# Decode attention with a gated MLP: four heads per load, 32 KB per partition, instead of one head per load

## The chip, the core and the metric

The kernel runs on one core of a Trainium2 chip. It is written by hand in instruction streams, one for each engine: TensorE (PE in the profile; PEld is its weight loads), VectorE (DVE), ScalarE (ACT), GpSimd (POOL) and SyncE (SP). The streams meet only at semaphores. SP, ACT and POOL also issue DMA transfers, which run on the core's 16 DMA engines. The metric is device time in microseconds, the median of several runs: lower is better.

## The reference

One token `x` of 512 features is decoded against a cache of 32 heads with 4096 keys and 4096 values of 128 features each (bfloat16), and goes through a small MLP. The two results are mixed by a gate:

```python
def _A_ref(x, k_cache, v_cache, wq, wo):          # wq 512x4096, wo 4096x512
    q = (x @ wq) per head                         # 32 heads of 128
    scores = jnp.einsum("bhqd,bhkd->bhqk", q, k) * (Dh ** -0.5)
    p = _softmax(scores, axis=-1)
    o = jnp.einsum("bhqk,bhkd->bhqd", p, v)
    return o.reshape(B, Sq, Hq * Dh) @ wo
...
def _B_ref(x, w1, b1, w2, b2):                    # w1 512x1376, w2 1376x512
    h = relu(x @ w1 + b1) ** 2
    return h @ w2 + b2
...
g = _sigmoid((x * gate_w).sum(-1, keepdims=True))
return g * a + (1 - g) * b
```

Every key and every value is used once. They are 67.1 MB of the 78.8 MB that the kernel reads.

## The kernel before, in words

**Tiling.** A head's 4096 keys lie on 128 partitions as 32 blocks of 128 keys: partition p holds keys 32p to 32p+31, which are 8 KB in a row in memory. One DMA loads one head's keys (1 MB, `load_k`, L259), one its values (`load_v`, L265). Keys have 8 buffers (`Kt`, NK), values 8 (`Vt`, NV).

**Scores** are made in two ways. DVE multiplies the first 16 blocks with the query, which `qb` holds alike on all partitions, and sums over the features (`ttr`, L631, one instruction per block, XB = 16). For the other 16 blocks PE transposes each block into PSUM (L428, banks `KP`), ACT copies eight of them at a time to SBUF (`evac`, L362), and PE multiplies each with the query as a column (`scores`, L439). DVE copies these 16 scores beside its own (`smax`, L637) and takes the maximum.

**Softmax.** For four heads at a time PE transposes the maxima (`max_rows`), DVE reduces them (`gmax`), PE spreads them again (`max_cols`), and ACT makes the exponentials and their sums (`exps`, L373).

**Values.** `pv` (L464) multiplies each of the 32 blocks of values with its column of exponentials, 32 matmuls with one column each. `den` sums the denominators, `norm` (L658) divides and applies the gate.

**Queries.** wq comes first, in four loads of 1 MB. `q_rows(c)` (L406) makes the queries of four heads as rows on all partitions (four matmuls of 512 columns), ACT copies them to `qb` (L354), `q_cols` (L414) makes the four columns, and DVE copies them to `qcol`. The columns of wq are done step by step along the heads; `q_rows(7)` is done near the 19th head.

**Output.** The rows of wo for heads 0 to 22 are brought into the room of wq once all queries are made (`s_qps`), as strips of rows: fourteen strips (`RUNS`) by POOL, each row in pieces of 8 KB, with small dummy loads between them (`xb<-in_B_w_dram`, L316), and five strips (`FIRST`) by SP. POOL then waits for the dummies and for `mlp_h`, clears `w1_sb` and builds the selection matrices in it (L326 to L334). `turn_a` and `spread_a` bring the outputs of the first heads into the order of these rows (head 23 has its own step, `out_x`, L532); `out_a` (L508) multiplies 23 of the 32 row groups on PE, `part_y` the other nine on DVE (L681), and `sum_y` adds them. Heads 24 to 31 go through `regroup` and `out_b` (L526). The MLP is `mlp_h` (L478, L482), `mlp` on DVE and `mlp_out` (L547). All sums meet in `acc`, four columns of 128. At the end DVE adds the bias, PE transposes the four columns into four rows (L594), DVE copies them, and SP sends them (L295).

**Order.** Every stream is a loop over the heads written out by hand. SP loads seven heads of keys, then values and keys in turn:

```python
for h in range(LAG):
    load_k(h)
for h in range(NH):
    load_v(h)
    if h + LAG < NH:
        load_k(h + LAG)
```

A load into a used buffer waits on SP until DVE and PE are done with the old keys (`s_sd`, `s_t`) or PE with the old values (`s_pv`), and all later loads wait behind it.

Of the kernel before, what the change touches and what calls it, by code (L numbers as in the profile page):

```python
# [5 lines left out]
def bass_gated_mix__gqa_block_cached__dense_activation_squared_relu__decode_kernel(  # L6
# [15 lines left out]

# [7 lines left out]
    NB = 32  # L35
# [7 lines left out]
    XB = 16  # L43
    YB = NB - XB
    HB = YB // 2
    NK = 8
    NV = 8
    NS = 12
    NE = 8
    G = 4  # L50
    NG = NH // G
    HPO = 8
    LAG = 7
    NA = 24
    TB = 8
    GS = [0, 8, 10]
    TD = 23
# [9 lines left out]
    HF = 20  # L67
# [26 lines left out]
    k_h = A_k_cache.rearrange("a h (p b) d -> (a h) p (b d)", p=128)  # L94
    v_h = A_v_cache.rearrange("a h (p b) d -> (a h) p (b d)", p=128)
    wq_v = A_wq.rearrange("(p t) n -> p t n", t=4)
    woa_v = A_wo.rearrange("(p t) n -> p (t n)", t=32)
    wob_v = A_wo[NA * 128:NH * 128, :].rearrange("(p t) n -> p (t n)", t=TB)
# [4 lines left out]
    with ctx:  # L103
# [8 lines left out]

        Kt = sb("Kt", [128, NK, NB * 128], bf16)
        Vt = sb("Vt", [128, NV, NB * 128], bf16)
# [3 lines left out]
        wox = Kt[:, 1, 0:DM]  # L118
        wob_sb = Kt[:, 0, :].rearrange("p (t n) -> p t n", t=TB)
        qb = sb("qb", [128, NH * 128], bf16)  # L120
        kT = sb("kT", [128, 2, YB * 128], bf16)
# [24 lines left out]
        E = sb("E", [128, NE, NB], bf16)  # L146
        mp = sb("mp", [128, NH], fp32)
        gm = sb("gm", [G, NG], fp32)
        dg = sb("dg", [G, NG, G], fp32)
        nM = sb("nM", [128, NH], fp32)  # L150
# [9 lines left out]
        hs = sb("hs", [128, FG + 1], bf16)  # L160
        b2g = sb("b2g", [128, 4], fp32)
        fin = sb("fin", [128, 4], bf16)

        KP = [pb(f"KP{i}", [128, HB * 128], bf16) for i in range(3)]
        pS = pb("pS", [128, 512], fp32)
        pM = pb("pM", [128, 512], fp32)
        pO = pb("pO", [128, 512], fp32)
        pX = pb("pX", [128, 512], fp32)
        pQ = pb("pQ", [128, 512], fp32)
        S2 = pS[:, 0:YB]  # L170
        O2A = pS[:, 64:96]
        O2B = pS[:, 128:128 + TB]
        o2D = S[:, NS - 1, 0:32 - TD]
        yD = kT[:, 0, 0:1024].bitcast(fp32)
        MT = pM[:, 0:128]
        MB = pM[:, 128:128 + NH]
        DEN = pM[:, 192:192 + NH]
        Z = pX[:, 0:1]
        XC = pO[:, 0:4]
        Q = pQ[:, 0:4]  # L180
        H = pX[:, 128:128 + FG + 1]
        acc = pX[:, 256:260]
        OB = [pO, pX, pO, pQ]

        def O(a, b):
            c = a // HPO
            return OB[c][:, 320 + a - HPO * c:320 + b - HPO * c]

        s_wr = sem("s_wr")
        s_wx = sem("s_wx")  # L190
        s_y = sem("s_y")
        s_y2 = sem("s_y2")
        s_x = sem("s_x")
        s_dz = sem("s_dz")
        s_b = sem("s_b")
        s_wq = [sem(f"s_wq{t}") for t in range(4)]
        s_w1 = sem("s_w1")
        s_w2 = [sem(f"s_w2{n}") for n in range(len(GS))]
# [3 lines left out]
        s_at = sem("s_at")  # L202
        s_ac = sem("s_ac")
        s_sb = sem("s_sb")
        s_b2 = sem("s_b2")
        s_oT = sem("s_oT")
        s_oc = sem("s_oc")
        s_o2 = sem("s_o2")
        s_fT = sem("s_fT")
        s_f4 = sem("s_f4")  # L210
        s_k = [sem(f"s_k{i}") for i in range(NK)]
        s_v = [sem(f"s_v{i}") for i in range(NV)]
        s_id = sem("s_id")
        s_cst = sem("s_cst")
        s_xc = sem("s_xc")
# [5 lines left out]
        s_g = sem("s_g")  # L221
        s_q = sem("s_q")
# [21 lines left out]
        s_hs = sem("s_hs")  # L244
        s_acc = sem("s_acc")
        s_fin = sem("s_fin")
        s_out = sem("s_out")

        nc.sync.dma_start(wq_sb[:, 0, :], wq_v[:, 0, :]).then_inc(s_wq[0], 16)
# [5 lines left out]
        def _(eng):  # L255
            for t in range(1, 4):
                eng.dma_start(wq_sb[:, t, :], wq_v[:, t, :]).then_inc(s_wq[t], 16)

            def load_k(h):  # L259
                if h >= NK:  # L260
                    eng.wait_ge(s_sd, h - NK + 1)
                    eng.wait_ge(s_t, 2 * (h - NK + 1))
                eng.dma_start(Kt[:, h % NK, :], k_h[h, :, :]).then_inc(s_k[h % NK], 16)  # L263

            def load_v(h):  # L265
                if h >= NV:
                    eng.wait_ge(s_pv, h - NV + 1)
                eng.dma_start(Vt[:, h % NV, :], v_h[h, :, :]).then_inc(s_v[h % NV], 16)  # L268

            for h in range(LAG):  # L270
                load_k(h)
            for h in range(NH):
                load_v(h)
                if h + LAG < NH:
                    load_k(h + LAG)
                if h == HF:
                    eng.wait_ge(s_qps, 8)
                if HF <= h < HF + len(FIRST):
                    p, st, k, q = STRIPS[len(RUNS) + h - HF]
                    eng.dma_start(W[p:p + st * (k - 1) + 1:st, :], woa_v[q:q + k, :],  # L280
                                  max_dma_last_dim=8192).then_inc(s_wr, 16)
                if h == 8:
                    eng.wait_ge(s_z, 1)
                    eng.wait_ge(s_b2, 1)
                    for t in range(4):
                        eng.dma_start(w1_sb[:, t, :], w1_v[:, t, :]).then_inc(s_w1, 16)
# [53 lines left out]
        def _(eng):  # L340
# [15 lines left out]
            def evac(h):  # L356
                if h >= 2:
                    eng.wait_ge(s_s2, h - 1)
# [29 lines left out]
        def _(eng):  # L388
# [43 lines left out]
            def scores(h):  # L432
                if h >= 1:
                    eng.wait_ge(s_cp, h)
# [318 lines left out]
```

## Time and profile before

| | |
|---|---|
| median of 3 runs | 196.97 us (196.86 to 197.03) |
| span of the profiled execution | 195.4 us, 6571 instructions |
| moved | 78.76 MB, 403 GB/s over the span |
| PE busy | 132.8 us (68%) |
| DVE busy | 139.5 us (71%) |
| ACT busy | 79.4 us (41%) |
| POOL busy | 29.9 us (15%) |
| DMA's share of the chain that ended last | 59% |

The profile gives the span of the profiled execution, from its first to its last instruction, and no other time of it: the runs' median stands 1.6 us above this span. The 40 slices of the page are 4.9 us each; a digit is the busy share in tenths. PEclk is the clock that TensorE was granted, in tenths. A group of instructions is given with its line, engine, operation, tiles and shapes, then its busy time, the mean nanoseconds of one, and the idle time of the engine just before them with what ended it. An issue of a DMA is given with its count, KB each and median time to landing.

### The profile page before, as it was taken

Reading aid. Unit: us, or ns where it says so; the run is one execution under the profiler, and the core shown is the slowest. Engines: PE = TensorE matmul, PEld = TensorE weight load, DVE = VectorE, ACT = ScalarE, POOL = GpSimd, SP = SyncE. Lnnn points to the kernel's source line nnn. Section 1 sums busy time; section 2 is a strip of 40 time slices with the busy share of each in tenths; the row PEclk is TensorE's granted clock in tenths of the full one; section 3 lists DMA queues with packets and bytes.
Section 4 is the critical chain, followed back from the end, with each engine's and each line's share of the span. In section 5 each row is a group of like instructions: output and inputs, shape, how many; then the busy total and the mean of one; then the engine's idle time right before and its main releaser. Section 6 shows DMA issues by size and latency. Waiting matters only on the chain.

```text
span 195.4 us, 6571 instructions
## 1 busy us (share of the span) xinstructions
PE 132.8 (68%) x2409; PEld 117.3 (60%) x2409; DVE 139.5 (71%) x1151; ACT 79.4 (41%) x148; POOL 29.9 (15%) x53
## 2 busy tenths in 40 slices
PE   0128657597986857906797771568998677787774
PEld 0106527476686647606667761568997667776664
DVE  0307999999998687707877773577769999958510
ACT  2105838456563536403347330633068333612000
POOL 2000000000000000000009950000089760000000
PEclk9999966667555665555555555555555555555555
DMA  6999999999999999999999999999999999999991
GB/s 227 420 426 424 424 418 424 411 421 426 416 411 423 418 421 407 420 421 421 418 421 419 411 416 416 406 409 413 408 419 421 426 409 421 419 423 414 416 382 57
DMA packets 12717, 78.76 MB, mean 403 GB/s; under 512 B 2489, under 2 KB 2715, under 8 KB 3356
## 3 DMA queue, kind: packets, MB, share of 16 engines
q1 hardware_dynamic: 11134, 75.77, 94.0%
q0 software_dynamic: 1536, 2.56, 3.5%
q8 instruction: 19, 0.31, 0.7%
q14 instruction: 14, 0.11, 0.2%
q10 hardware_dynamic: 14, 0.01, 0.0%
HBM read 78.32 MB, written 0.00 MB: 401 GB/s over the span
## 4 chain that ended last, share of the span: by engine, by line
DMA 59%; DVE 22%; PE 9%; SPq 6%; issue 3%; ACT 0%
DMA Kt<-in_A_k_cache_dram 42%; DVE Kt L631 19%; DMA w2a<-in_B_w_dram 12%; DMA W<-in_A_wq_dram 6%; SPq L268 4%; PE KP L428 3%; PE pX L482 2%; DVE S L631 1%; SPq L263 1%; PE pQ L406 1%; PE pX L478 1%; PE pX L547 1%; PE pS L439 1%; DVE dg L646 1%; DVE S L637 0%
## 5 line engine op out<-in xcount | busy, mean ns | idle before, releaser
L631 DVE CUSTOM_DVE_ANT_0 Kt<-Kt,qb 128x128 bf16<-128x128 bf16 x512 | 113.3, 290 | 23.4 <-DMA Kt<-in_A_k_cache_dram 23.4
L362 ACT ACTIVATE kT<-KP 128x1024 bf16<-128x1024 bf16 x64 | 61.8, 1021 | 68.4 <-PE KP L428 68.4
L428 PE MATMUL KP<-ident,Kt 128*128 128x128 bf16 x512 | 55.2, 294 | 32.0 <-DMA Kt<-in_A_k_cache_dram 32.0
L428 PEld LDWEIGHTS KP<-ident,Kt 128*128 128x128 bf16 x512 | 47.9, 137 | 34.4 <-DMA Kt<-in_A_k_cache_dram 33.6
L631 DVE DVE_READ_ACCUMULATOR2_ANT S<- 128x1 f32 x512 | 41.4, 81 | 0.0
L439 PE MATMUL pS<-qcol,kT 128*128 128x1 bf16 x512 | 19.0, 167 | 11.1 <-DVE S L637 11.1
L439 PEld LDWEIGHTS pS<-qcol,kT 128*128 128x128 bf16 x512 | 18.4, 106 | 13.2 <-DVE S L637 13.2
L316 POOL DMA_DIRECT2D xb<-in_B_w_dram x9 | 5.3, 592 | 100.3 <-PE pQ L406 100.3
L406 PE MATMUL pQ<-W,xb 128*128 128x512 bf16 x32 | 14.5, 609 | 6.4 <-DMA W<-in_A_wq_dram 6.4
L464 PEld LDWEIGHTS pO<-E,Vt 128*128 128x128 bf16 x512 | 15.4, 104 | 1.1 <-issue 0.8
L464 PE MATMUL pO<-E,Vt 128*128 128x1 bf16 x512 | 16.0, 165 | 0.0
L334 POOL TENSOR_SCALAR_AFFINE_SELECT w_sb<-w_sb 24x36 bf16<-24x36 bf16 (+5 forms) x19 | 11.0, 577 | 2.7
L354 ACT ACTIVATE qb<-pQ 128x512 bf16<-128x512 f32 x8 | 4.7, 591 | 14.8 <-PE pQ L406 14.8
L406 PEld LDWEIGHTS pQ<-W,xb 128*128 128x128 bf16 x32 | 3.6, 130 | 10.9 <-issue 10.9
L373 ACT ACTIVATE E<-S,nM 128x32 bf16<-128x32 f32 x32 | 9.9, 309 | 0.3
L464 PE MATMUL pQ<-E,Vt 128*128 128x1 bf16 x256 | 8.1, 165 | 2.3 <-DMA Vt<-in_A_v_cache_dram 2.0
L464 PEld LDWEIGHTS pQ<-E,Vt 128*128 128x128 bf16 x256 | 7.7, 104 | 2.6 <-issue 2.5
L464 PEld LDWEIGHTS pX<-E,Vt 128*128 128x128 bf16 x256 | 7.9, 105 | 0.7 <-issue 0.6
L464 PE MATMUL pX<-E,Vt 128*128 128x1 bf16 x256 | 8.1, 166 | 0.0
L319 POOL DMA_DIRECT2D W<-in_A_wo_dram x14 | 7.8, 563 | 0.0
L617 DVE CAST qcol<-pQ 128x4 bf16<-128x4 f32 x8 | 1.2, 152 | 8.5 <-PE pQ L414 8.5
L637 DVE COPY S<-pS 128x16 f32<-128x16 f32 x32 | 5.4, 169 | 2.2 <-PE pS L439 2.2
(85 smaller groups left out, 93.5 us busy)
## 6 DMA issues: line engine op xcount, KB each, us to landing
Kt<-in_A_k_cache_dram SPq DMA_DIRECT2D x32, 1024.0 KB, 27.1
Vt<-in_A_v_cache_dram SPq DMA_DIRECT2D x32, 1024.0 KB, 27.2
W<-in_A_wq_dram SPq DMA_DIRECT2D x4, 1024.0 KB, 7.8
W<-in_A_wo_dram POOLq DMA_DIRECT2D x2, 768.0 KB, 13.0
w_sb<-in_B_w_dram SPq DMA_DIRECT2D x4, 344.0 KB, 22.9
Kt<-in_A_wo_dram SPq DMA_DIRECT2D x1, 1024.0 KB, 21.5
w2a<-in_B_w_dram SPq DMA_DIRECT2D x1, 1024.0 KB, 23.4
W<-in_A_wo_dram POOLq DMA_DIRECT2D x10, 64.0 KB, 23.4
```

The source lines that it names most:

```text
L268: eng.dma_start(Vt[:, h % NV, :], v_h[h, :, :]).then_inc(s_v[h % NV], 16)
L316: eng.dma_start(dm[0:d, sent, :, 0:8], src[:, :, 0:8]).then_inc(s_dm[sent], 16)
L319: eng.dma_start(W[p:p + st * (k - 1) + 1:st, :], woa_v[q:q + k, :], max_dma_last_dim=8192).then_inc(s_wp[n], 16)
L334: eng.affine_select(out=part, in_=part, compare_op=ALU.not_equal, fill=1.0, base=-st * q, pattern=[[st, 4], [-1, st * (k - 1) + 1]], chann ...
L362: eng.activation(kT[:, h % 2, j * HB * 128:(j + 1) * HB * 128], KP[n % 3][:, :], ACT.Copy).then_inc(s_ev, 1)
L373: eng.activation(E[:, h % NE, :], S[:, h % NS, :], ACT.Exp, bias=nM[:, h:h + 1], scale=SCALE, accum_out=RS[:, h:h + 1]).then_inc(s_e, 1)
L406: mm = eng.matmul(pQ[:, :], xb[:, t, :], wq_sb[:, t, c * 512:(c + 1) * 512], start=(t == 0), stop=(t == 3))
L428: mm = eng.transpose(KP[n % 3][:, y * 128:(y + 1) * 128], Kt[:, h % NK, b * 128:(b + 1) * 128], ident[:, :])
L439: mm = eng.matmul(S2[:, y:y + 1], kT[:, h % 2, y * 128:(y + 1) * 128], qcol[:, h:h + 1], start=True, stop=True)
L464: mm = eng.matmul(O(h, h + 1), Vt[:, h % NV, b * 128:(b + 1) * 128], E[:, h % NE, b:b + 1], start=(b == 0), stop=(b == NB - 1))
L631: ins = eng.tensor_tensor_reduce(kb, kb, qb[:, h * 128:(h + 1) * 128], 1.0, 0.0, ALU.mult, ALU.add, S[:, h % NS, b:b + 1])
L637: eng.tensor_copy(S[:, h % NS, XB:NB], S2).then_inc(s_cp, 1)
```

## The change

**Loads.** One DMA loads the keys (or values) of four heads, a quad: head r of the quad lies on partitions 32r to 32r+31, and each partition holds 128 keys in a row, 32 KB. There are 8 quads. One tile `KV` has 4 slots of 32 KB per partition, as much as `Kt` and `Vt` had together: keys go through slots 0 to 2, values through slot 3 alone, but for the last two quads of values, which take slots 2 and 0. The first quad of keys is loaded in four parts, the second in two, the last quad of values in four. The rest of SP's order is in the diff.

**Scores.** DVE takes 14 of each 32 blocks (XB), PE the other 18, in nine groups of eight per quad. A transposed block now has the keys of all four heads; PE multiplies it with four columns at once, and ACT copies from each row group its own head's column (`s_copy`). Exponentials are written with zeros for the other heads, so that `pv` multiplies 128 blocks with four columns each.

**Order.** PE works on group g of a quad and the scores of group g-2; the values of quad q-2 are multiplied after the scores of quad q. Query columns 1 and 2 follow quad 0, 3 to 5 lie in quad 1, 6 and 7 in quad 2 (`Q_AT`). wq comes as its first 512 columns, ahead of the keys, and the rest behind the first quad of keys. POOL's strips follow `q_rows(7)` as before. `mlp_h` follows quad 4.

**End.** `part_y` and `sum_y` are gone; `out_a` does all 32 row groups on PE, ahead of the last quad of values. The last two groups of w2 are multiplied by PE as rows (`mlp_rows`, with `hd` holding the four copies of a column among zeros), in the shape of the output: `acc` with the bias is turned into rows by one FP32 matmul and added to them in PSUM, and DVE copies the rows out.

```diff
-    XB = 16
-    NK = 8
-    NV = 8
-    LAG = 7
-    TD = 23
+    R = 4
+    NQ = NH // R
+    NB = 128
+    NP = 4
+    XB = 14
+    GB = 8
+    GQ = YQ // GB
+    K_PARTS = [[1, 1, 1, 1], [2, 2]] + [[4]] * (NQ - 2)
+    V_PARTS = [[4]] * (NQ - 1) + [[1, 1, 1, 1]]
+    K_SLOT = [q % 3 for q in range(NQ)]
+    V_SLOT = [3] * (NQ - 2) + [2, 0]
+    W2_PARTS = [(0, 4), (4, 8), (FG, FG + 1), (8, 9), (9, 10)]
...
-    k_h = A_k_cache.rearrange("a h (p b) d -> (a h) p (b d)", p=128)
-    v_h = A_v_cache.rearrange("a h (p b) d -> (a h) p (b d)", p=128)
+    k_q = A_k_cache.rearrange("a (q r) (p b) d -> (a q) (r p) (b d)", r=R, p=32)
+    v_q = A_v_cache.rearrange("a (q r) (p b) d -> (a q) (r p) (b d)", r=R, p=32)
...
+            def load_k(q):
+                if q >= 3:
+                    eng.wait_ge(s_sd, q - 2)
+                    eng.wait_ge(s_t, GQ * (q - 2))
+                load(KV, k_q[q, :, :], K_SLOT[q], K_PARTS[q], s_k[q])
+            def load_v(q):
+                if V_SLOT[q] == 3:
+                    if q >= 1:
+                        eng.wait_ge(s_pv, q)
+                else:
+                    eng.wait_ge(s_sd, q)
+                    eng.wait_ge(s_t, GQ * q)
+                load(KV, v_q[q, :, :], V_SLOT[q], V_PARTS[q], s_v[q])
...
+            load_k(0)
+            eng.dma_start(wq_sb[:, :, 512:4096], wq_v[:, :, 512:4096]).then_inc(s_wq[1], 16)
+            load_k(1)
+            load_k(2)
+            load_v(0)
+            eng.wait_ge(s_z, 1)
+            eng.wait_ge(s_b2, 1)
+            eng.dma_start(w1_sb[:, :, :], w1_v[:, :, :]).then_inc(s_w1, 16)
+            for q in range(3, NQ):
+                load_k(q)
+                if q >= 4:
+                    load_first(q - 4)
+                load_v(q - 2)
+            load_first(4)
+            load_v(NQ - 2)
+            load_w2(0)
+            load_v(NQ - 1)
+            eng.wait_ge(s_sd, NQ)
+            eng.wait_ge(s_t, GQ * NQ)
+            eng.dma_start(wob_sb, wob_v).then_inc(s_wo, 16)
+            load_w2(1)
             eng.dma_start(wox, A_wo[HX * 128:NA * 128, :]).then_inc(s_wx, 16)
+            load_w2(2)
+            load_w2(3)
+            load_w2(4)
...
+        Q_AT = {1: (0, GQ - 1), 2: (0, GQ - 1), 3: (1, 0), 4: (1, 3), 5: (1, 6), 6: (2, 0), 7: (2, 3)}
...
+            def s_copy(q):
+                eng.wait_ge(s_s2, GQ * (q + 1))
+                S2 = pS[q % 2][:, 0:YQ * R].rearrange("p (b r) -> p b r", r=R)
+                for r in range(R):
+                    eng.activation(S[rows(r), q % NS, 0:YQ], S2[rows(r), :, r], ACT.Copy).then_inc(s_cp, 1)
...
+            def pv(q):
+                if q >= 1:
+                    eng.wait_ge(s_on, q)
+                else:
+                    eng.wait_ge(s_bg, 1)
+                for j in range(NP):
+                    eng.wait_ge(s_v[q][part_of(V_PARTS[q], j)], 16)
+                    for b in range(PB * j, PB * j + PB):
+                        mm = eng.matmul(O[:, R * q:R * q + R], KV[:, V_SLOT[q], b * 128:(b + 1) * 128],
+                                        E[:, q % NE, COLUMN[b], :], start=(b == 0), stop=(b == NB - 1))
                 mm.then_inc(s_pv, 1)
...
+            def mlp_rows(c):
+                eng.wait_ge(s_w2[c], 16)
+                n = W2_PARTS[c][0]
+                for j in range(4):
+                    mm = eng.matmul(acc4, hd[:, n - 8, 4 * j:4 * j + 4], w2a[:, n, j * 128:(j + 1) * 128],
+                                    start=(n == 8 and j == 0), stop=(n == FG - 1 and j == 3),
+                                    skip_group_check=True)
+                return mm
...
+            for q in range(NQ):
+                for g in range(GQ):
+                    transposes(q, g)
+                    if g >= 2:
+                        scores(q, g - 2)
...
+                scores(q, GQ - 2)
+                scores(q, GQ - 1)
...
+                if q >= 2:
+                    den(q - 2)
+                    pv(q - 2)
+                if q == 4:
                     mlp_h()
+            max_rows(NQ - 1)
+            turn_a()
+            max_cols(NQ - 1)
+            spread_a()
+            den(NQ - 2)
+            pv(NQ - 2)
+            eng.wait_ge(s_hs, 2)
+            out_a()
+            mlp_out(0)
+            den(NQ - 1)
+            pv(NQ - 1)
             regroup()
             out_b()
+            mlp_out(1)
             out_x()
+            mlp_out(2, last=True)
+            eng.wait_ge(s_hs, 3)
+            mlp_rows(3)
+            eng.wait_ge(s_as, 1)
+            eng.matmul(acc4, accs[:, :], identf[:, :], start=False, stop=False, skip_group_check=True)
+            mlp_rows(4).then_inc(s_fin, 1)
```

## The prediction

> **What bounds the kernel now.** I read the page first (busy shares, slices, queues, chain, groups, DMA issues), then the waits of all engines and of SP, then the timeline at the start, around 57 us and at the end, and last the windows.
>
> The slices, and the DMA queues under them:
>
> ```profile
> DVE  0307999999998687707877773577769999958510
> PEclk9999966667555665555555555555555555555555
> DMA  6999999999999999999999999999999999999991
> GB/s 227 420 426 424 424 418 424 411 421 426 416 411 423 418 421 407 420 421 421 418 421 419 411 416 416 406 409 413 408 419 421 426 409 421 419 423 414 416 382 57
> ...
> DMA packets 12717, 78.76 MB, mean 403 GB/s; under 512 B 2489, under 2 KB 2715, under 8 KB 3356
> ...
> q1 hardware_dynamic: 11134, 75.77, 94.0%
> q0 software_dynamic: 1536, 2.56, 3.5%
> ```
>
> Nothing between the first and the last two slices is below nine tenths on the DMA row: the time is one unbroken stream of 78.76 MB at about 420 GB/s, and the kernel ends when its slowest DMA engine ends. No compute engine is the bound: PE is 68% busy, DVE 71%, ACT 41%.
>
> The groups that the change moves, the waits, and the DMA issues:
>
> ```profile
> L631 DVE CUSTOM_DVE_ANT_0 Kt<-Kt,qb 128x128 bf16<-128x128 bf16 x512 | 113.3, 290 | 23.4 <-DMA Kt<-in_A_k_cache_dram 23.4
> L362 ACT ACTIVATE kT<-KP 128x1024 bf16<-128x1024 bf16 x64 | 61.8, 1021 | 68.4 <-PE KP L428 68.4
> L428 PE MATMUL KP<-ident,Kt 128*128 128x128 bf16 x512 | 55.2, 294 | 32.0 <-DMA Kt<-in_A_k_cache_dram 32.0
> ...
> L373 ACT ACTIVATE E<-S,nM 128x32 bf16<-128x32 f32 x32 | 9.9, 309 | 0.3
> ```
>
> ```profile
> POOL xb L316 <- PE pQ L406: 100.3, 1, 100.3
> ...
> POOL w_sb L326 <- DMA xb<-in_B_w_dram: 27.0, 1, 27.0
> ```
>
> ```profile
> Kt<-in_A_k_cache_dram SPq DMA_DIRECT2D x32, 1024.0 KB, 27.1
> ...
> xb<-in_B_w_dram POOLq DMA_DIRECT2D x3, 0.2 KB, 24.1
> ```
>
> A K load lands 27.1 us after its issue because some 11 MB are queued ahead of it: that depth is what keeps the stream unbroken, and the change spends it. And a 0.2 KB load from POOL takes 24.1 us to land: it takes turns with the SP queue.
>
> The end of the timeline:
>
> ```profile
> 186.94 0.93 PEld L464 LDWEIGHTS pQ<-E,Vt 128*128 128x128 bf16 x32
> ...
> 193.47 0.16 DVE L719 TENSOR_TENSOR fin<-pX,b2g 128x4 bf16<-128x4 f32 x1 [3.77 <-PE pX L547]
> ...
> 194.23 0.29 SPq L295 DMA_DIRECT2D out_dram<-fin  x1
> ```
>
> The last head's values are used from 186.94, and the output leaves 7.29 us later.
>
> **The sum is made against** the profiled span, 195.4 us; the median of the runs is 196.97, so 1.6 us lie outside the span and are carried over. A change within 0.2% (0.4 us) can't be told from none.
>
> **1. Fewer descriptors.** Let a packet cost o plus its bytes times x. Queue shares times 16 engines times 195.4 us give 11134 o + 75.77 MB x = 2938.8 us and 1536 o + 2.56 MB x = 109.4 us: x is 26.7 GB/s per engine, o 8.7 ns (7.3 to 10.1 within the rounding of the 3.5%). The packet records agree: 4 bytes take 9 ns, 8 KB 309 to 312. Per engine, K and V fall from 512 descriptors to 184 (32 for K0, 16 for K1, 32 for the last V in quarters, 8 for each other quad); wq rises from 32 to 64 (its 512 first columns are 1 KB rows); w1 falls from 32 to 8; w2a rises from 16 to 32. That is 304 fewer, and some 36 fewer DMAs with one completion write per engine: 340 x 8.7 ns = 2.9 us shorter (2.5 to 3.4). No row has a descriptor above 8 KB on this queue; if 32 KB cost as much per byte as 8 KB the gain is 0, and that end is kept. I take 2.9, since o was the same from 4 bytes to 8 KB.
>
> [...]
>
> **2. Values have one buffer.** V0 to V5 share slot 3, so the load of V(q) waits on SP for pv(q-1) (s_pv); behind it in SP's order stand K(q+3) and a strip of wo. K3, V1, K4, V2 ... alternate, each 4.19 MB, 9.75 us. From a K quad's last byte to the bytes of the next V that waits on it:
> - last byte to semaphore: about 1.0 us (wq's 4.19 MB from 2.2 at 422 GB/s end at 12.1; PE starts at 13.2);
> - K work: 72 transposes at 105 ns (16 take 57.77 to 59.45 at half clock) and 72 score matmuls at 29 ns are 9.7 us of PE. ACT: nine copies at 0.93 us (four run in 3.74), nM 0.18, four exponentials at 0.40 (0.31 for 32 columns plus 96 columns at the copy's 0.83 ns, an estimate), behind a first group of 1.0 and before the last scores' 0.4: 11.8 us. ACT's chain ends last;
> - den 0.4, pv 128 x 26 ns (32 take 0.83): 3.7;
> - SP issue to first bytes: 1.5 (issue at 0.74; the first slice moved 1.1 MB, so bytes from 2.2).
>
> 18.0 us against 19.5 for two loads: in the steady state hidden, with 1.5 us left. Three places are not steady:
> - V1. Stream ends: wq's first columns 3.6, K0 13.6, rest of wq 22.4, K1 32.1, K2 41.9, V0 51.6, w1 55.0, K3 64.7. PE: quad 0 to about 20; query columns 1 and 2 wait for wq, 23.4 to 29.9; quad 1 also carries three q_rows (1.66 us each at half clock) with four ACT copies behind each (0.26, between the 4- and 512-column rows): 14.8 us at full clock, 17.5 at half; quad 2 with two: 13 to 16.5. pv(0) ends between 61.5 and 67.6, V1's bytes come at 63 to 69, K3 ends at 64.7: 0 to 4.4 us idle. I take 1.2: the granted clock is 1 until 24 us and between 0.5 and 1 until 47.
> - Skew. Only engines without other work idle there: POOL's strips (2.56 MB, now after q_rows(7) at about 53 us instead of 102) fill the gap on the engines that they fall on. They are uneven: in the trace's semaphore records the sixteen increments of one K load lie 0.4 us apart early and 9.3 us apart at 128 us, while strips land. The engines with few strips run ahead. Today's depth forgives that; with one V buffer an engine more than about 3.5 us ahead of the slowest (9.75 less 1.0, 3.7 and 1.5) waits. 0 to 2 us, I take 0.5.
> - mlp_h, 5.15 us of PE (136.03 to 141.18), stands between pv(2) and quad 5: it uses the 1.5 spare and may cost up to 1.5; I take 0.
>
> Together 1.7 us of idle stream (0 to 6).
>
> **3. Engines.** DVE: 448 instead of 512 products at 0.2125 us pitch, 13.6 us less; part_y goes (6.7 us); its S and qcol copies go to ACT, whose busy time rises from 79 to about 98 us. Beside the stream; uncovered, they'd be the chain under 2. max_cols waits for gmax, which stands behind one quarter of products (3.0 us) on DVE, ready at 3.9 us into a quad and wanted at 5.5: nothing. smax waits for ACT's S copies, with the next quad's products behind it: DVE has 6 us per cycle free.
>
> **4. Start and end.** The first load has 512 descriptors instead of 128; its issue took 0.39 us: 0 to +0.5, I take 0.2. XC no longer waits for gate_w; hidden by the stream. End: behind the last V, 2.59 MB (6.16 us) become 2.06 MB (4.9), as w2's first half went ahead. PE from the last V: 2.82 us to out_b (as 186.94 to 189.76), 32 + 16 + 8 matmuls 1.45, accs 0.4, the FP32 matmul 0.25, four 128-column matmuls 0.6, copy 0.25: 5.9 us to the output's issue, so 1.0 after the stream's end, against 7.29 - 6.16 = 1.1 now. The transpose and copy of fin go, but the chain ahead is now as long as the stream. 0, within 0.4 either way. out_a's 36 more matmuls (0.95 us) lie beside the last V.
>
> **Sum.** 195.4 - 2.9 + 1.7 + 0.2 = 194.4; with 1.6 outside, **196.0 us**.
>
> **Rivals.**
> - *No idle (0.13).* pv(0) ends by 63.2: full clock from 24 us on. For it: warm stretches (0.85 to 1.0) at 33 to 36 and 43 to 46. Against: half clock from 47 in nearly all slices. 193.8 to 195.0.
> - *One V buffer costs more than the descriptors save (0.27), the other side.* Place: SP's wait for s_pv at V1, again at V3 and V4. Each microsecond of pv(0) past 63.2 is one of idle; from 2.7 us (pv(0) past about 66) it's slower. The half-clock sums end there. Price up to 6: 197.4 to 200.
> - *POOL's queue starves (0.13).* q0's 96 packets per engine (1536/16) took from 106 to 142 us, as many turns as q1's 8 KB descriptors in that time, 0.31 us each. Behind 32 KB a turn is 1.2 us: 96 are 117 us, from 60 to 177. POOL then needs 18.6 us (142.3 to 160.8) before spread_a, with pv(6), out_a and pv(7) behind it on PE, some 16 us: span up to 210. It decides if the last dummy lands after about 148, as spread_a comes at about 167. Against: whenever q1 idles, at V1, q0 drains at 9 ns to 0.3 us a packet. 200 to 211.
> - *32 KB rows bring nothing (0.04):* sum 198.9.
>
> [...]
>
> **How the numbers follow.** Forecast 0.43, 195.0 to 197.1. Of it 0.36 is faster by over 0.2% and 0.07 within; with *no idle* faster is 0.49; within 0.2% 0.09 (0.02 from the slower side's edge); slower 0.42. Range 193.8 to 201.5: it holds all but the low edge and most of the starved case, about 0.13.
>
> **What would show it.** Right: part 3 with about 5,400 fewer q1 packets, and GB/s of 427 to 431 where only 32 KB rows move; DMA digits below nine near 65 us; SP waiting on PE's pv at V1. Wrong: GB/s still 420 (step 1); more idle slices (step 2); POOL waiting for xb beyond 90 us and PE idle at spread_a (starving); output leaving over 1.6 us after the last weights (step 4).

## The result, and the profile after

The changed kernel takes 202.17 us (median of 4 runs, 201.65 to 202.54) against 197.0 us before (196.86 to 197.03): a ratio of 1.026, 95% interval 1.024 to 1.028. It is slower, by 5.2 us, where 196.0 was forecast and 201.5 was the end of the range. The profiled span grew from 195.4 to 200.4 us. Two of the six runs of one variant below (`late_first_pad`, 203.76 and 203.91 us) count as slow and stand outside its figures.

The slices, packets and queues of the page after; a slice is 5.0 us here:

```profile
DMA  5999999999899999999999999997999999999930
GB/s 191 414 426 395 441 432 448 441 448 419 373 469 420 349 386 424 435 432 435 432 435 415 370 422 425 428 345 342 451 417 441 432 415 420 405 410 422 399 113 0
DMA packets 7147, 78.75 MB, mean 393 GB/s; under 512 B 1785, under 2 KB 2779, under 8 KB 3548
...
q1 hardware_dynamic: 5566, 75.76, 90.3%
q0 software_dynamic: 1536, 2.56, 3.6%
```

The first reading goes well: 5568 packets fewer on q1, 348 for each engine where the prediction counted 340, and 432 to 448 GB/s from 20 to 45 us, where large rows move; in the kernel before no slice passed 426. (The packet records say the same: 32 KB take 1.213 us, 432 GB/s over 16 engines; 8 KB take 0.309 us, 424 GB/s.) But the row has dents that were not there before: 349 (the 14th slice, 65 to 70 us), 370 (110 to 115), 345 and 342 (130 to 140); 373 in the 11th is made up for by 469 in the 12th. And the last slice is empty: the stream is over and the kernel goes on.

The end of the timeline after (start, busy time, engine, line, count; in brackets the idle time before the group and what ended it):

```profile
177.40 3.56 PE L528 MATMUL pO<-E,KV 128*128 128x4 bf16 x128 [0.60 <-DMA KV<-in_A_v_cache_dram]
...
181.26 0.70 PE L566 MATMUL pQ<-o2A,W 128*128 128x1 bf16 x21 [0.30 <-issue]
184.00 2.99 PE L566 MATMUL pQ<-o2A,W 128*128 128x1 bf16 x107 [2.04 <-issue]
...
187.71 0.19 PE L528 MATMUL pO<-E,KV 128*128 128x4 bf16 x2
...
190.54 3.50 PE L528 MATMUL pO<-E,KV 128*128 128x4 bf16 x126 [2.64 <-issue]
...
199.22 0.30 SPq L332 DMA_DIRECT2D out_dram<-fin  x1
```

The last quarter of the values lands at 188.5 us and the last row of w2 at 193.6 (by the DMAs' semaphore records, as are all landings below). Yet `pv(7)` ends only at 194.0, and the output leaves at 199.22, 5.6 us behind the last landing; before it was 1.2 (193.0 and 194.23). In that tail PE stands still twice in the middle of a run of equal matmuls, 2.04 us behind the 21st of `out_a` and 2.64 us behind the 2nd of `pv(7)`, and the profile names no releaser: "issue". Such a wait is called a hole below. Before, the longest that PE's own rows show on L464, the same work, was 0.4 us (time in total, how often, the longest):

```profile
PE pQ L464 <- issue: 0.4, 1, 0.4
```

So the 5.0 us more of span are 0.6 us in the stream (last landing 193.0 to 193.6) and 4.4 us behind it.

The trace's packet records show one more thing. The queue of instructions (q8) moves packets of 16,384 bytes. After 160 us they start at

```
164.90   174.60   181.38   187.95   191.64   195.37
```

Two of them lie beside the two holes (181.96 and 187.90), and PE goes on 2.6 us after the start of each. Between the holes lie 107 + 16 + 2 + 2 = 127 matmuls, each with its weight load, and two waits: 256 instructions, 64 bytes each if they fill one packet. At that size the 5218 records of PE's instructions are 20.4 packets, and q8 moved 20 of them; before it was 19.3 and 19. So q8 is read as the queue of PE's program. The first theory follows: **PE waits for its own code.** A run of 256 instructions takes PE 3.55 us (the 128 matmuls of one `pv`), while from the end of the first hole to the end of the second 6.5 us pass. Rival: there is simply too much matmul work behind the last values.

For the stream the theory was that ACT's row of work stands ahead of the release of the one buffer of values; its rival, that handing over a single buffer costs its latency each time.

### The profile page after: what moved, and what is told of

Same layout as the page of the kernel before. It is cut to its first block, busy times and chain, and to the rows that moved or that the text cites. A ratio compares the mean times of both kernels' runs of the same rounds, so it can differ in the third digit from the quotient of the medians.

```text
span 200.4 us, 6656 instructions
## 1 busy us (share of the span) xinstructions
PE 128.1 (64%) x2546; PEld 113.4 (57%) x2550; DVE 111.8 (56%) x958; ACT 106.5 (53%) x220; POOL 30.9 (15%) x56
## 4 chain that ended last, share of the span: by engine, by line
DMA 47%; PE 24%; ACT 18%; issue 8%; SPq 2%; DVE 0%; ACTq 0%; DVEq 0%
DMA KV<-in_A_k_cache_dram 24%; DMA KV<-in_A_v_cache_dram 12%; ACT kT L407 11%; DMA W<-in_A_wq_dram 11%; PE pO L528 9%; PE KP L483 5%; PE pQ L467 4%; ACT E L425 4%; ACT qb L396 4%; PE pQ L566 2%; SPq L274 1%; PE pS L495 1%; PE pM L517 1%; PE pQ L584 1%; PE pQ L600 0%
## 5 line engine op out<-in xcount | busy, mean ns | idle before, releaser
L705 DVE CUSTOM_DVE_ANT_0 KV<-KV,qb 128x128 bf16<-128x128 bf16 x448 | 98.9, 284 | 39.1 <-DMA KV<-in_A_k_cache_dram 35.9
L483 PE MATMUL KP<-ident,KV 128*128 128x128 bf16 x576 | 54.1, 258 | 13.3 <-DMA KV<-in_A_k_cache_dram 13.3
L483 PEld LDWEIGHTS KP<-ident,KV 128*128 128x128 bf16 x576 | 44.6, 118 | 16.0 <-DMA KV<-in_A_k_cache_dram 13.8
L495 PE MATMUL pS<-qcol,kT 128*128 128x4 bf16 x576 | 26.1, 167 | 27.9 <-ACT kT L407 27.5
L705 DVE DVE_READ_ACCUMULATOR2_ANT S<- 128x1 f32 x448 | 33.4, 75 | 0.0
L528 PEld LDWEIGHTS pO<-E,KV 128*128 128x128 bf16 x1024 | 29.1, 105 | 6.5 <-issue 6.5
L528 PE MATMUL pO<-E,KV 128*128 128x4 bf16 x1024 | 28.6, 166 | 6.3 <-DMA KV<-in_A_v_cache_dram 3.7
L425 ACT ACTIVATE E<-S,nM 32x128 bf16<-32x128 f32 x32 | 18.5, 577 | 0.9
L396 ACT ACTIVATE qb<-pQ 32x128 bf16<-32x128 f32 x32 | 8.6, 267 | 13.9 <-PE pQ L467 13.3
L425 ACT ACTIVATION_READ_ACCUMULATOR E<-S,nM 32x1 f32 x32 | 8.0, 250 | 0.0
```

The source lines that it names most:

```text
L396: eng.activation(qb[rows(r), c, :], pQ[rows(r), r * 128:(r + 1) * 128], ACT.Copy)\
L425: eng.activation(E[rows(r), q % NE, :, r], S[rows(r), q % NS, :], ACT.Exp, bias=nM[rows(r), q:q + 1], scale=SCALE, accum_out=RS[rows(r), h ...
L483: mm = eng.transpose(KP[n % 3][:, y * 128:(y + 1) * 128], key(q, b), ident[:, :])
L495: mm = eng.matmul(pS[q % 2][:, R * c:R * c + R], kT[:, n % NT, y * 128:(y + 1) * 128], qcol[:, R * q:R * q + R], start=True, stop=True)
L528: mm = eng.matmul(O[:, R * q:R * q + R], KV[:, V_SLOT[q], b * 128:(b + 1) * 128], E[:, q % NE, COLUMN[b], :], start=(b == 0), stop=(b == N ...
L705: ins = eng.tensor_tensor_reduce(key(q, b), key(q, b), qb[:, q, :], 1.0, 0.0, ALU.mult, ALU.add, S[:, q % NS, c:c + 1])
```

## Experiments on the tail: whose time is it?

In all of this section a time stands beside runs of the kernel before on the same chip, 196.84 to 196.95 us. Executions of the changed kernel and its variants spread over up to 2.4 us (before: 0.4), so less than 1 us between two of its members is not read as a difference without an interval.

**Fewer instructions, the same PE time.**

```diff
-                for t in range(32):
-                    for j in range(4):
-                        eng.matmul(acc[:, j:j + 1], wo_sb[:, t, j * 128:(j + 1) * 128],
-                                   o2A[:, t:t + 1], start=(t == 0 and j == 0), stop=False,
-                                   skip_group_check=True)
+                for j in range(4):
+                    eng.matmul(acc[:, j:j + 1], wo_sb[:, 0, j * 128:(j + 1) * 128], o2A[:, 0:1],
+                               start=(j == 0), stop=False, skip_group_check=True)
+                for t in range(8):
+                    eng.matmul(pS[0][0:32, :], o2A[:, :], wo_sb[:, t, :], start=True, stop=True)
```

> The part of wo that covers heads 0 to 23 is worked out in 12 matmuls (four of 1 column, eight of 512 columns) instead of 128, so the output lacks 31 of its 32 terms per column; TensorE's time for it stays about the same (8 x 0.43 us at the 0.5 clock of this stage = 3.4 us, against 3.6 us), its instructions fall from 256 to 24. Theory, TensorE waits for its own code: two stretches of 2.04 us (at 181.96) and 2.64 us (at 187.90), in which the page names no releaser, each begin within 0.6 us of a 16 KB packet on the queue of instructions. With 232 instructions fewer in this place one of the two waits goes and the other falls where TensorE waits for values anyway: values times E of the last group ends about 1 us after its last part lands (188.5), and the kernel takes 198.0 to 199.0 us. Rival, TensorE's work in the tail is simply too much: the same 3.4 us lie in the same place, no change, 201.5 to 202.5.

Measured: 200.18 us (198.73 to 200.21), 2.0 us faster, between the two forecasts. The eight wide matmuls took 3.59 us, so PE's work was the same, and of the two holes one was left. The gain is the tail's: the last row of w2 landed 0.6 us later than in the changed kernel (194.2), and the output left 3.4 us behind it instead of 5.6. The place of the hole that was left, in the timeline:

```profile
186.55 3.33 PE L528 MATMUL pO<-E,KV 128*128 128x4 bf16 x118
...
192.06 0.41 PE L528 MATMUL pO<-E,KV 128*128 128x4 bf16 x10 [2.18 <-issue]
```

116 matmuls fewer stand ahead, and the hole moved from behind the 2nd to behind the 118th matmul of `pv(7)`: exactly 116. The rival falls; the theory's size was wrong, because the hole did not land in a wait for values but 10 matmuls ahead of the end.

**The same instructions in another order.**

```diff
             spread_a()
             den(NQ - 2)
-            pv(NQ - 2)
             eng.wait_ge(s_hs, 2)
             out_a()
+            pv(NQ - 2)
             mlp_out(0)
```

> The changed kernel with one exchange in TensorE's order: the 128 matmuls of the output for heads 0 to 23 come ahead of the values of group 6 instead of behind them. Theory, TensorE is paced by its own code from 171 us on (about 6.2 us for each 256 instructions of a stretch that runs at full speed): their number is the same, and only the wait for the values of group 6 (1.1 us, from 176.24 to 177.40) is filled, so 200.5 to 201.8 us. Rival, the two waits without a releaser belong to the place (the row of wo or the order of the accumulations) and not to the code: they go, 197.5 to 199.0.

Measured: 202.13 us (201.0 to 202.47), no change. The timeline:

```profile
177.38 3.56 PE L566 MATMUL pQ<-o2A,W 128*128 128x1 bf16 x128 [0.31 <-issue]
...
180.79 0.70 PE L528 MATMUL pO<-E,KV 128*128 128x4 bf16 x21
...
184.03 2.99 PE L528 MATMUL pO<-E,KV 128*128 128x4 bf16 x107 [2.54 <-issue]
...
187.74 0.19 PE L528 MATMUL pO<-E,KV 128*128 128x4 bf16 x2
...
190.58 3.50 PE L528 MATMUL pO<-E,KV 128*128 128x4 bf16 x126 [2.65 <-issue]
```

`out_a` now runs through, and the holes stand behind the 21st matmul of `pv(6)` and the 2nd of `pv(7)`: the same numbers in the stream, other work, and the same times (184.03 and 190.58 against 184.00 and 190.54). A hole belongs to a place in the stream of instructions and not to what is executed there. The time lies 0.3 us above the theory's range. `out_a` started at 177.38, with 0.31 us of waiting ahead of it, so there was less to fill than the 1.1 us of the expectation, and the next code did not come sooner.

**Work ahead of the last values.** The late exponentials (next section) let PE reach `out_a` at about 171 us, while the values of quad 6 land at 175; with the exchanged order `out_a` leaves the crowded stretch.

> The exponentials behind the key copies and, with them, the 128 matmuls of the output for heads 0 to 23 ahead of the values of group 6. In the run with the late exponentials alone TensorE was ready for these matmuls at 170.2 us and waited 4.4 us for the values of group 6, which landed at 175.0. Theory: 256 instructions leave the stretch behind 175.0, and the code for the rest comes in while parts of the last values land (to 186.2); values times E of the last group ends by about 188.5, the last rows of w2 land at 191.3, the output leaves 1 to 2.5 us behind them: 195.2 to 197.0 us. Rival, the tail hangs on the chain behind the last values (5.2 us from the end of values times E to the output) and on single waits for code wherever they fall: 198.0 to 199.9.

Measured: 197.40 us (196.12 to 198.0, 10 runs), ratio to before 1.0025 (1.0008 to 1.0042), 4.8 us faster than the changed kernel and 0.4 us above the theory's range. The timeline of the profiled execution, which took 196.12:

```profile
171.24 3.55 PE L572 MATMUL pQ<-o2A,W 128*128 128x1 bf16 x128 [0.40 <-issue]
...
177.18 3.00 PE L534 MATMUL pO<-E,KV 128*128 128x4 bf16 x107 [1.32 <-issue]
...
183.18 2.65 PE L534 MATMUL pO<-E,KV 128*128 128x4 bf16 x94 [2.10 <-issue]
...
186.24 1.01 PE L534 MATMUL pO<-E,KV 128*128 128x4 bf16 x32 [0.41 <-DMA KV<-in_A_v_cache_dram]
...
189.37 0.54 PE L581 MATMUL pS<-oB,w_sb 8*128 8x8 bf16 x15 [0.99 <-issue]
...
193.53 0.30 SPq L332 DMA_DIRECT2D out_dram<-fin  x1
```

The last quarter of `pv(7)` now waits for its values (186.24), and the output leaves 2.2 us behind the last row of w2 (191.3). The late exponentials alone left 5.3 us there, so the instructions moved out of the stretch are worth 3 us of the tail.

**Moving the holes.** One hole of 0.99 us is left in `regroup`, on the path. 36 matmuls of one element, ahead of the wait for wq at the start (`late_first_pad`), should put every hole 72 instructions, 36 matmuls, earlier in PE's work.

```diff
+            for n in range(36):
+                eng.matmul(pM[0:1, 300:301], ident[0:1, 0:1], ident[0:1, 0:1], start=True, stop=True)
             eng.wait_ge(s_wq[0], 16)
```

> The run with the late exponentials and the exchanged order, with 36 more matmuls of one element each at its start, where TensorE waits 2.8 us for wq; nothing reads them. In that run TensorE waited 0.99 us without a releaser between the first and second of the 16 matmuls that regroup the last heads, on the path to the output, 252 instructions behind such a wait in the last values times E. Theory, these waits stand at every 256th instruction of TensorE's stream: 72 instructions ahead of them the last one falls into the last values times E, where TensorE waits for the landing at 186.2 us anyway, so 0.6 to 1.2 us faster, 196.2 to 196.8 us, although TensorE has more to do. Rival, the waits hang on what is executed there and not on its place in the stream: no change, 197.1 to 197.7 us.

> The same 36 matmuls in the run that has the contiguous E as well (1.44 us of that wait in the same place). Theory: 0.8 to 1.6 us faster than without them, 196.4 to 197.2 us. Rival: no change, 197.9 to 198.2 us.

Measured: 199.97 us (199.91 to 200.19, 4 runs) and 200.07 us (199.79 to 200.29), 2 to 3 us slower instead of 1 us faster. One thing that had happened is not about code: POOL's selects came late and VectorE beside them was slow (last section). A wait moved on POOL takes this away:

```diff
-            for n in range(sent):
-                eng.wait_ge(s_dm[n], 16)
             eng.wait_ge(s_h, 1)
             eng.memset(w1_sb[0:NA, 0:3, 0:1024], 0.0).then_inc(s_sb, 1)
...
+            for n in range(sent):
+                eng.wait_ge(s_dm[n], 16)
```

> The run with the late exponentials and the exchanged order, with one wait moved on POOL: it waits for its dummy transfers into xb behind its memset and selects, not ahead of them. In that run the memset started at 135.0 us, released by the last dummy; with the 36 added matmuls the dummy came only at 156.2 us and VectorE's products of the last keys, 213 ns apart before, came up to 2 us apart beside the selects. Theory: the selects start behind the hidden layer's matmuls, at about 113 us, beside the products of group 5, and the wait for the next keys (5.9 us from 127.9) takes what they cost: 197.0 to 198.0 us, no change. Rival: beside the products of group 5 they hold up the release of a key buffer, 0.5 to 2 us slower.

> The 36 added matmuls and the moved wait together. Theory: the 2.7 us that the added matmuls cost came from POOL's late selects alone and not from the places where TensorE waits for code; with the selects at about 113 us what was expected of them shows, no wait inside the regrouping: 0.6 to 1.2 us faster than the run before it, 196.2 to 197.0 us. Rival: TensorE's waits in their new places (behind matmul 114 of the output for heads 0 to 23, behind 113 of group 6) cost as much as the old one: 197.2 to 198.0.

> As before, with the contiguous E. Theory: ACT is off the path here, so the same within 0.5 us, 196.0 to 197.0. Rival: it is still on the path in some groups, 0.5 to 1.5 us faster than without.

Measured: without the added matmuls 196.81 us (196.56 to 198.04), ratio to before 1.0005 (0.999 to 1.0021), no loss beside the products of quad 5; with them 199.78 us (199.72 to 199.81), and 199.86 with the contiguous E. So the late selects were worth 0.2 us of the padded kernel's loss, and the added matmuls still cost 3.0 us. The timeline with them:

```profile
170.93 0.28 PE L556 MATMUL KP<-ident,onorm 128*24 128x128 bf16 x1 [1.75 <-issue]
...
178.98 0.54 PE L574 MATMUL pQ<-o2A,W 128*128 128x1 bf16 x14 [2.84 <-issue]
...
185.26 0.54 PE L536 MATMUL pO<-E,KV 128*128 128x4 bf16 x15 [2.74 <-issue]
...
191.01 1.04 PE L536 MATMUL pO<-E,KV 128*128 128x4 bf16 x34 [1.84 <-issue]
...
197.22 0.29 SPq L332 DMA_DIRECT2D out_dram<-fin  x1
```

The holes moved as the theory says: behind matmul 114 of `out_a`, 113 of `pv(6)` and 94 of `pv(7)`, each 35 or 36 matmuls earlier, and `regroup` has none. What failed is the sum of their price. The hole at 170.93, ahead of `out_a`, now starts a row of blocks of 256 instructions that follow each other at 8.0, 6.3 and 5.8 us, and the whole row is late. I read it so that holes cannot be moved one by one; what ties a block to the one before, and why the first distance is 8.0 us, is not shown. The rival expectation, that the new places cost as much, was nearer, and too low as well.

## Experiments on the stream: descriptors and the one buffer

**Descriptors alone.** All loads of keys and values cut at 8 KB.

```diff
-                    eng.dma_start(dst[:, slot, a:b], src[:, a:b]).then_inc(s, 16)
+                    eng.dma_start(dst[:, slot, a:b], src[:, a:b], max_dma_last_dim=8192).then_inc(s, 16)
```

> The changed kernel with its loads of keys and values cut into descriptors of 8 KB. Theory, the saving of descriptors is real and lies on the path: 1664 descriptors of 32 KB become 6656, 312 more per DMA engine x 8 ns = 2.5 us; where the stream waits for the one buffer of values a part of this hides, so 203.2 to 204.7 us. Rival, the kernel's end hangs on the engines alone and not on the stream: under 0.6 us more, 201.8 to 202.8. Rival, larger descriptors brought nothing: no change.

Measured: 204.59 us (203.98 to 204.90), 2.4 us slower than the changed kernel; the last row of w2 lands at 196.2 instead of 193.6, 2.6 us later. The page counts 12,395 packets, 5248 more, 328 per DMA engine: 7.4 ns each by the time, 7.8 by the landing. The packet records agree: four packets of 8 KB at 309 ns take 1236 ns, one of 32 KB takes 1213, so 7.7 ns for each of the three more. The saving is real and on the path.

**The exponentials behind the key copies.**

```diff
             def exps(q):
                 eng.wait_ge(s_mb, q + 1)
                 eng.activation(nM[:, q:q + 1], MB[:, q:q + 1], ACT.Copy).then_inc(s_nm, 1)
+
+            def exponentials(q):
                 eng.wait_ge(s_nm, q + 1)
...
                 s_copy(q)
+                if q >= 1:
+                    exponentials(q - 1)
```

> The four exponentials of a group move from the middle of the next group's key copies (after the sixth of nine) to behind them and the copy of the scores, on ACT. Theory, ACT's row of work stands before the release of the buffer of values: 4 x 0.83 us = 3.3 us leave the stretch from a group's keys to its values, so the stream's gaps (3.7 us in all) fall to under 1 us, and in the tail the values of group 5 are taken 2.5 us earlier, when they land; 195.8 to 198.5 us. Rival, the gaps come from the latency of handing over one buffer and the tail from TensorE alone: 0 to 1.5 us better, 200.7 to 202.5.

Measured: 199.87 us (199.17 to 201.09), 2.3 us faster, between the two forecasts. The stream did what the theory says. V1 to V4 are issued at 67.58, 87.21, 106.95 and 130.18 us instead of 68.60, 88.51, 111.60 and 133.69; the DMA engines' unused time between 8 and 188 us (no packet under way, by the packet records; mean over 16 engines) falls from 1.31 to 0.05 us; what packets of 32 KB take beyond their usual 1.213 us in the ten microseconds around each dent (66 to 76, 108 to 118, 128 to 138 us) falls from 0.58 + 0.49 + 0.87 = 1.9 us to 0.6; and the last row of w2 lands at 191.3 instead of 193.6. `pv(3)` and the issue of V4 that it releases, in the changed kernel and then here:

```profile
130.10 3.55 PE L528 MATMUL pO<-E,KV 128*128 128x4 bf16 x128
133.69 0.34 SPq L274 DMA_DIRECT2D KV<-in_A_v_cache_dram  x1
```

```profile
129.05 1.09 PE L534 MATMUL pO<-E,KV 128*128 128x4 bf16 x35 [1.06 <-issue]
130.18 0.34 SPq L274 DMA_DIRECT2D KV<-in_A_v_cache_dram  x1
```

The tail did not follow: 5.3 us against 5.6. `pv(5)` ran 6.0 us earlier, but `out_a` still stood behind `pv(6)`, whose values came at 175.

**E written contiguously.**

```diff
-        E = sb("E", [128, NE, NB, R], bf16)
+        E = sb("E", [128, NE, R, NB], bf16)
...
-                    eng.activation(E[rows(r), q % NE, :, r], S[rows(r), q % NS, :], ACT.Exp,
+                    eng.activation(E[rows(r), q % NE, r, :], S[rows(r), q % NS, :], ACT.Exp,
...
-                                        E[:, q % NE, COLUMN[b], :], start=(b == 0), stop=(b == NB - 1))
+                                        E[:, q % NE, :, COLUMN[b]], start=(b == 0), stop=(b == NB - 1))
```

> E is kept by head and block (written contiguously by ACT) instead of by block and head (written 8 bytes apart); TensorE reads its four columns 256 bytes apart. Theory, the spacing makes the exponentials 0.58 us long where 0.40 was estimated: they fall to about 0.40, 0.7 us less per group, 200.0 to 201.5 us. Rival, the spacing costs ACT nothing: the exponentials stay at 0.58 us and the time at 202.2 within 0.4. Rival, TensorE reads spaced columns slower: a pass of 128 matmuls takes longer than 3.43 us and the time goes up.

Measured: 199.85 us (198.94 to 201.36), 2.3 us faster. The groups of the changed kernel, then of this one (mean ns of one is the number behind the bar's first comma):

```profile
L425 ACT ACTIVATE E<-S,nM 32x128 bf16<-32x128 f32 x32 | 18.5, 577 | 0.9
L425 ACT ACTIVATION_READ_ACCUMULATOR E<-S,nM 32x1 f32 x32 | 8.0, 250 | 0.0
```

```profile
L425 ACT ACTIVATE E<-S,nM 32x128 bf16<-32x128 f32 x32 | 12.7, 398 | 0.9
L425 ACT ACTIVATION_READ_ACCUMULATOR E<-S,nM 32x1 f32 x32 | 5.9, 184 | 0.0
```

By these records writing 8 bytes apart costs 179 ns in the exponential and 66 ns in reading out its sum. But the two overlap, so their times may not be added. Two exponentials of one quad with the read-out between them, in the changed kernel and then here:

```profile
164.79 0.58 ACT L425 ACTIVATE E<-S,nM 32x128 bf16<-32x128 f32 x1
165.12 0.26 ACT L425 ACTIVATION_READ_ACCUMULATOR E<-S,nM 32x1 f32 x1
165.40 0.57 ACT L425 ACTIVATE E<-S,nM 32x128 bf16<-32x128 f32 x1
```

```profile
100.29 0.40 ACT L425 ACTIVATE E<-S,nM 32x128 bf16<-32x128 f32 x1
100.60 0.18 ACT L425 ACTIVATION_READ_ACCUMULATOR E<-S,nM 32x1 f32 x1
100.81 0.40 ACT L425 ACTIVATE E<-S,nM 32x128 bf16<-32x128 f32 x1
```

They start 0.61 us apart, and 0.52 with the contiguous E: 0.4 us per quad, not the 0.7 expected. (So the late exponentials took 2.4 us per quad out of the stretch, not 3.3.) PE's reads got no slower: a `pv` takes 3.55 us as before. As with the late exponentials the gaps close (0.23 us unused) and the last row of w2 lands at 191.5. V1 is issued 1.3 us earlier and V4 3.0, more than ACT saves by itself; an earlier quad lets the next one begin earlier, but how much of the 2.3 us comes in this way is not shown. Two different changes of ACT's work close the same gaps: ACT's row ahead of `pv` is on their path.

**Both together, with the exchanged order.**

> As the run before, and E written contiguously. Theory: with ACT's work already behind the release of the buffer of values, the 1.0 us per group that the contiguous E saves is off the path: within 0.7 us of the run with the late exponentials and the exchanged order, 194.8 to 196.8. Rival, the release of the buffer still waits for ACT in some groups: 1.0 to 2.3 us faster than that run.

Measured: 198.02 us (197.92 to 198.23), 0.6 us slower than without the contiguous E, and above the theory's range; in its profiled execution the values of quad 6 landed at 176.65 instead of 175.0. With the moved selects:

> The late exponentials, the exchanged order, POOL's moved wait and the contiguous E, without the added matmuls. Theory: ACT is no longer on the path, and the 0.6 us by which the contiguous E was slower together with the late exponentials came from POOL's selects beside the products of group 6; with the selects beside group 5 it comes out within 0.6 us of the run without the contiguous E, 196.2 to 197.4 us. Rival, the contiguous E itself costs time once ACT is off the path (TensorE's reads or a shifted wait for code): 197.5 to 198.5.

Measured: 196.91 us (196.32 to 198.13, 12 runs), ratio to before 1.0011 (0.9994 to 1.0027); quad 6 lands at 175.3. So the contiguous E itself costs nothing, and gains nothing once ACT is off the path. That POOL's selects beside the keys of quad 6 made the difference fits, but with executions that spread over 1.8 us it is not shown.

No version beats the kernel before: the best two lie on it, with intervals that end at 1.0021 and 1.0027.

## Why the prediction was wrong, step by step

**Step 1, fewer descriptors, -2.9: right.** Cutting them back costs 2.4 to 2.6 us; per descriptor 7.4 to 7.8 ns against 8.7 taken, 348 of them instead of 340.

**Step 2, one buffer of values, +1.7: right in kind, short in size, and the place was wrong.** With step 1 and a start that is 0.5 us later (unused engine time in the first 8 us, 1.94 before and 2.43 after, where step 4 took 0.2), the stream should end at 193.0 - 2.6 + 0.5 = 190.9; it ended at 193.6, 2.7 us of gaps. Unused time and slow packets around the dents together give 1.3 + 1.9 = 3.2. The term that was mis-sized most is the four exponentials: taken at 0.40 us, they start 0.61 us apart, 2.4 us instead of 1.6 per quad. From the landing of the keys of quad 4 to the end of `pv(2)` 17.0 us passed (94.6 to 111.6). The prediction has 15.5 for it (its 11.8 of ACT is 11.6 by its own terms), so the exponentials are half of what was missing; the first six copies (6.0 us instead of 5.6) and `pv` (3.55 instead of 3.3) are most of the rest. V1 cost 0.6 us, by its slow packets, not 1.2, and that by luck: `pv(0)` ended at 68.6, behind the whole range from 61.5 to 67.6, but the keys of quad 3 landed late as well, at 68.8 instead of 65.7 (64.7 and 1.0 to the semaphore). The most was lost at V4, 0.9 us in slow packets and 1.1 us of unused time. Ahead of it `mlp_h` kept PE until 116.7 us, 2.6 us past the landing of quad 5's keys (114.1), and the prediction had given it 1.5 us of spare time and a price of nothing. With the late exponentials it ended at 112.2, ahead of the keys (113.8), and the gap was gone; no run moved `mlp_h` alone, so its share in V4's gap is argued.

**Step 3, engines, nothing: half right.** DVE came out at 111.8 us, where the terms give 112.6 (139.5 - 13.6 - 6.7, and 6.6 of copies that went to ACT). ACT came out at 106.5 instead of 98; 32 exponentials at 0.61 instead of 0.40 us are 6.7 of that. But "beside the stream" held for the sums only. ACT's part that stands ahead of each `pv` was the chain under step 2.

**Step 4, start and end, +0.2 and 0 within 0.4: the end is where the forecast broke, 4.4 us.** The step counted PE's work behind the last values at some 26 ns for each matmul, without a wait between them, and put the 36 more matmuls of `out_a` beside the last values. The matmuls did take that (128 in 3.55 us). The sign that the prediction gave for this step, the output more than 1.6 us behind the last weights, showed: 5.6 us. What the step left out is that 485 matmuls, 970 instructions, stand between the landing of quad 6's values (177.3) and the output, and that 256 instructions came only every 6.5 us, where PE runs them in 3.55. Values by quads bunch this work: `pv(6)` cannot start before all 4 MB of its values are there, and `out_a` and `pv(7)` follow at full speed. With the tail as before, 200.4 - 4.4 = 196.0 of span and 1.6 outside would have been 197.6 us: inside the range, but 0.3% slower than before and not faster, by step 2. Of the 6 us between forecast and result this step holds some four and a half, step 2 about one; the start and the descriptors share the rest.

**The rivals.** *One buffer costs more than the descriptors save* had the right sign: the gaps and the later start, 3.2 us, against 2.6 saved, 0.6 us slower by themselves. Its place, V1 at half clock, was not the main one. *POOL's queue starves* did not decide: its last dummy came at 115.1 us, ahead of `mlp_h`, which released the selects at 117.0; the gaps had drained the queue, as was argued against it. Close the gaps, and it comes back (below). *No idle* and *32 KB rows bring nothing* fall.

## What to carry to other kernels

Count instructions as well as engine time: where a stretch of one engine runs hundreds of short instructions without a wait, and the profile shows holes that it puts down to issue, look whether they stand 256 instructions apart and beside a 16 KB packet on the queue of instructions, as two do here (181.96 and 187.90 us, the packets at 181.38 and 187.95). Here work moved to where the engine waits anyway was worth 2.5 us (199.87 to 197.40), fewer instructions 2.0, and another order alone nothing. And when a buffer's depth is given up, every engine whose work stands ahead of its release can be on the path, as ACT was here (2.3 us); cost each row of it (here exponentials with a spaced write and a read-out) with the shape that it will have, and take the distance of starts from a timeline, as the records of one engine can overlap (here a read-out that starts at 165.12 us, in an exponential that ends at 165.37).

## What the hardware showed that was not expected

**Code.** The holes above. PE goes on 2.6 us after the start of the packet (184.00 and 190.54 after 181.38 and 187.95). Under 8 KB descriptors the holes end 6.3 us apart (186.37 and 192.64) against 6.5 under 32 KB, so the size of the data's descriptors is not what sets the distance. While the stream runs out two packets start 3.7 us apart (187.95 and 191.64). The packets start behind the end of a hole, by 1.1 us (190.54, 191.64) to 3.95 (184.00, 187.95) here and up to 5.6 (170.93, 176.50) in `late_first_pad_sel`. What sets the delay, and whether other traffic does, was not tried and stays open.

**A queue that moves in another's gaps.** POOL's strips were issued by about 69 us in all of these kernels, 96 packets for each DMA engine. In the changed kernel the last dummy landed at 115.1 us: by the packet records 31 of the 96 moved from 70 to 80 us and 13 from 110 to 120, beside two of the dents, and 5 in each 10 us between. With the gaps closed some 7 moved in each 10 us, in which the other queue has room for 8 packets of 32 KB at 1.213 us, and the last dummy released POOL's memset only at 135.0 (`late_first`). With the keys and values cut at 8 KB, 23 moved from 80 to 90 us, and the last dummy landed at 95.9. So here POOL's packets take turns with those of the other queue, about one for one, and the size of those sets the pace. With the 36 matmuls the memset came at 156.2, though 95% of the packets had moved by 140; why the last few took so long is not shown:

```profile
POOL w_sb L366 <- DMA xb<-in_B_w_dram: 87.0, 1, 87.0
```

**VectorE beside GpSimd.** When the selects came that late (159 to 172 us; in `late_first` they ended at 153) they ran beside the products of the last keys. The windows of `late_first` and then of `late_first_pad`, DVE's busy time and, in brackets, its instructions:

```profile
158.00:162.00 4.00, 4.00 (x38) 1.00 0.98 422
162.00:166.00 4.00, 4.00 (x39) 0.72 0.96 410
```

```profile
158.00:162.00 4.00, 3.97 (x20) 0.90 0.99 422
162.00:166.00 4.00, 4.00 (x30) 0.95 0.98 418
```

DVE is busy all the time in both, and gets through 20 and 30 instructions instead of 38 and 39; single products last up to 2.1 us instead of 0.27. PE waited 4.2 us for the maxima of the last quad. With the memset at 114.7 us and the selects behind it (`late_first_pad_sel`) that wait was 0.6 us. Why DVE gets through fewer instructions beside the selects is not shown.
